# Sorted-block attention and a two-layer FFN in one kernel: seven pairs of output tiles by seven block products, scores on 64-row tiles, and the last chunk in two halves

## The chip, the cores and the metric

The kernel runs on one core of a Trainium2 chip. The metric is the device time in microseconds of one execution. The core has five instruction streams that run beside each other and wait for each other by semaphores: TensorE (PE, matmuls, with its weight loads listed as PEld), VectorE (DVE), ScalarE (ACT), GpSimd (POOL, which here also issues the loads) and SyncE (SP, which issues stores and DMA transposes).

## What is computed

```python
# q, k, v: (4, 8, 768, 64); sort_net: (4, 8, 8, 8)
P = sort_net
for _ in range(5):                       # row and column normalisation
    P = P - max(P, -1);  P = exp(P)
    P = P / (sum(P, -1) + 1e-9);  P = P / (sum(P, -2) + 1e-9)
k_sorted = einsum('bhij,bhjcd->bhicd', P, k_blocks)    # 8 blocks of 96 rows
v_sorted = einsum('bhij,bhjcd->bhicd', P, v_blocks)
scores = q_block @ k_sorted_block.T / 8                # within each block of 96
attn = softmax(scores) @ v_sorted_block                # (4, 8, 768, 64)
x = attn, heads side by side                           # (3072, 512)
h = x @ w_in                                           # w_in (512, 2048)
g = max(h, 0) + alpha * min(h, 0)                      # alpha (2048,)
out = g @ w_out                                        # w_out (2048, 512), float32
```

## The kernel before

**The work.** There are 32 attention groups g (4 batches b of 8 blocks i, 96 tokens, all 8 heads). Batch 0 is prepared in its own way; for batches 1 to 3 the sorted K and V come from matmuls against block-diagonal matrices (`prep_k` at L672, `prep_v` at L713) whose weights POOL or ACT lay out first (`conv_k` at L659, `conv_v` at L405, into the zero-padded buffers KSz and VDz). `attention` makes the scores of 8 heads (L763 in batch 0, L760 in the others), the row maxima on DVE (L769), the exponentials on ACT (L797), turns them by a DMA transpose, multiplies with V (L817), scales (L830) and turns the result into xT, the tokens as columns.

**Scores.** In batch 0 a head takes 64 rows of the matrix: two heads stand one above the other (`hp`), so the eight matmuls are four pairs on 64-row tiles. In batches 1 to 3 the two heads of a pair share the keys' 128 rows, and q is stored twice as wide, with zeros in the half of the other head (QN, zeroed by eight POOL memsets at L495; QTz by DMA transposes of 128x1024, L443): eight matmuls of all 128 rows.

**FFN.** The first layer runs in chunks of tokens: two of 192, then seven of 384. A step `ffn1` (L879) makes one of 16 blocks of 128 features (four matmuls of 384 columns; in a chunk of 192 two blocks, eight matmuls of 192), alternately into the two banks of psH; ACT (L889) and DVE (L893) apply the activation and write hT, a ring of 768 tokens. The second layer makes 24 tiles of 128 tokens. A plain tile (`ffn2`, L919) is 16 matmuls of 512 columns into one bank, a copy on ACT or DVE, and a store. A **pair** of tiles (`strassen`) is a 2x2 block product by seven products instead of eight: the blocks are the two tiles, the even and odd feature blocks, and the two halves of the 512 columns. Eight sums S of hT blocks (L994, 128x512 each, on DVE or POOL), seven products of eight matmuls of 256 columns (L1013, in two halves of four), three snapshots of partial sums (L405 into `sn`), three totals (L1027) and two stores. `w_sums` (L957) makes eight sums of w_out blocks once. PAIRS is [13, 16, 19, 22]: tiles 13, 14, 16, 17, 19, 20, 22 and 23 go by pairs, the other 16 by the plain form.

**Order.** No engine's order comes from the program text. `SEQ` is one written list of operation numbers (`_Graph` numbers them as they are added); each engine takes its operations in the list's order. A letter behind a number names the engine where there is a choice (p POOL, a ACT, d DVE; without a letter, the first of the choices: DVE for S and w_out sums, ACT for copies). `i4H` and the like are warming matmuls (L1172). `arrange` works out start times by the program's own cost figures, and `emit` places the waits that the data need.

```python
PAIRS = [13, 16, 19, 22]
SMALL = ("dve", "pool")
chunks = [(0, 2), (2, 4)] + [(c, c + 4) for c in range(4, NG, 4)]
```

Of the kernel before, what the change touches and what calls it, by code (L numbers as in the profile page):

```python
# [7 lines left out]
AP = bass.AP  # L8
# [13 lines left out]
RING = 768  # L22
# [10 lines left out]
0 18 1 4 2 7 3 8 42 43 25 10 44 5 33 40 45 46 24 11 37 47 6 48 49 14 50 51 39 52 28 53 9 54 23 55 i1P 143 56  # L33
57 i4H 26 58 29 127 59 60 61 62 21 63 126 64 41 65 66 22 85 67 128 68 87 69 83 88 70 13 71 i6Y 72 86 73 74 75
129 16 76 77 78 134 79 81 80 130 34 82 96 89 12 38 91 90d 94 95 97d 144 92 98 140 100 84 i9Y 20 101 136 103a
102d 104 17 99d 107a 110 93d 106 105d 111 145 112 108a 146 114 109 154 115 113d 147 15 155 116 148 137 120
117d 118 156 139 119 121d 122 35 157 19 132 124 123d 135 i3Y 125 27 133 158 149 159 i4G 150 160d 151 179 161
180 i2H 152 162d 153 181 36 163 182 188 164 165 166 196 189 205 190 197 192 206 183 191 193 198 207 194 209
184 195 199 185d 213 210 208 186 211 214 221 212 233 187 217 222 138 244 218 215 30 216 200 245 167p 223 201
219 232 202d 248 224 230 246 203 220 142 204 247 266 249 267 258 231 237 234 250 259 251 268 235 141 260 168  # L40
225 269 262 131 261 226 238 227d 263 252 236 239 264 241 286 315d 289 276 228 265 242 305 243 240 253 306 229
280 290 270 279 277 271 293 291 278 272d 287 307 294 292 173 275 295 273 308 170 274d 285 281 297 288 282d 314
296 342 174 283 343 309 284 301 298 310 175 316 311d 302 344 317 299 300 312 345 303 320 313d 328 326 304 321
323d 346 329 332 32 347 169p 348d 324 333 254 353 319 330 331 349 334 255 171p 350 367 335 325 318 382 256 392
383 322 351 393 395 384 394 336 31 352d 365 337 366 357 396 385 416 327 397 398 417 419 399 257 338 176 420
418 400 421 355 422 356d 425 358d 423 339 426 424 428 401 340 427 359 446 354 360d 449 429 447 361 450 368
362d 430 408 451 369 448 409 363 455 364d 431 411 458 456 452 459 410 177 386 453 370 387 457 460 439 388d 371
454 389 479 390d 372 461 402 414 403 488 443 415 404d 476 178 489 480 405 412 477 440 512 406 481 490 438 478
432 485 441d 413 482 433 434d 486 469 513 491 483 487 435 442 484 444 436 509 445d 472 462 510 524 463 506
464d 378 511 470 507 465 377 514 471 466d 508 374 521 525 518 380 522 492 523 519 515 375 526 493 520 379 545  # L50
516d 474 381 542 475 527 560 376 546 554 561 543 468 341 555 544 562 547 473 500 548 501d 499 551 494d 563 502
552 498 556 503d 549 553 535 589 557 550 534 391 590 504 577 505 558d 437 580 578 495 579 581 538 625 591 571
407 496d 582 572 583 533 537 528 586 529 584 530d 536 539 626 585 587 540 569 588 592 531 541 622 532 570d 575
631 623 573 624 627 600 574 172 632 576 598 634 599 601 564 635 602 608 565 628 633 603 610 636 637 609 629
566d 497 606 604 638 655 605d 607 517 639 567 640 373 568d 649 641 611 593 650 652 612 594 595d 656 653 651
642 596 657 597d 654 613 661 643 664 662 667 663 665 658 559 666 684 668 659 676 687 685 696 686 688 677 669
689 697 711 682 690 680 670 702 691 678 693 703 698 467 694 679 683d 704 644 695 699 810 645 692 712 722 646d
660 700 705 713 681 731 714 719 732 723 817 717 720 751 724 744 733 721 728 812 671 725 715 672 729 673d 734
766 718 745 730 752 726 767 647 816 742 706 753 727 618 768 707 674 708d 757 716 743d 748 740 758 754 749 759
741 801 750 755 746 630 621 802 763 747 769 735 619 764 760 736 737d 709 789 776 761 765 803 762 790 813 738  # L60
775 783 777 811 784 786 778d 615 836 785 787 791 620 788 779 792 614 780d 837 795 781 804 793 782d 796 797 798
770 830 799 838 800 814 815d 818 821 819 617 839 771 616 844 944p 772d 822 845 820 773 831 864 823 824 825 847
865 756 827 805 848 648 832 945p 826 828 829 866 875 849d 852 855 833 806 807d 851 853 846 872 840 850 874 856
873 854 857 858 834d 876 710 861 859 877 883 841 675 878 860 862 863 952p 948p 879 880 842d 867 889 701 890
898 774 881 899 884 891 885 868 739 900 953 808 895 950p 882 954p 869 886 924 896 887 843 870d 892 949p 925
912 893 913 871 926 901 897 894 955p 909 910 906 835 982 911 962 921 907 908 927 951p 922 983 923 918 914 919
984 902 956 957p 920 903 794 963 935 915 1002 936 904d 937 1003 916 932 928 933 1004 960 961 934 941 938 942
958p 929 959p 964d 930d 965 966 943 967 946p 939 1022 968 940 993 985 990 1023 969 888 994 986 991 995 1024
992 905 970 972d 809 999 996 947p 987 971 931 997 988d 973 974 1000 1068p 1048 998 1010 1001 917 1013 1069p
975 1011 1014 976 1049 1005 1006 978 1076 1015 1070p 1012 979 1050 1007 1019 1020 980 1016 1008d 1021 1025 989  # L70
1017 1036 1026 1018 1009 1098 1099 977 1033 1034 1030 1031 1035 1032 1027 1071p 1037 1028d 1038 1042 1100 1043
1045 1044 1046 1039 1072p 1118 1056 1040 1051 1073p 1047 1119 1059 1074p 1077 1057 1052 1078 1060 1058 1062
1075 1061 1053 1080 1101 1079 1054d 1041 1065 981 1063 1082 1083 1120 1066 1102 1081 1064 1084 1088d 1106 1107
1067 1089 1121 1090 1109 1110 1108 1111 1091 1103 1112 1029 1085 1086 1113 1168p 1087 1114 1115 1104d 1126
1116 1117 1127 1144 1128 1105 1122 1123 1129 1124d 1130 1132 1133 1145 1131 1134 1055 1135 1092 1136 1138 1137
1146 1141 1094 1095 1169p 1125 1139 1142 1140 1150 1143 1153 1151 1154 1172p 1147 1152 1148 1155 1170p 1156
1157 1159 1096 1174p 1158 1160 1176 1161 1177 1162 1180 1165 1163 1182 1164 1166 1167 1171p 1178 1097 1179
1173p 1198 1199 1181 1201 1183 1228 1200 1202 1203 1204 1188d 1207 1205 1184 1208 1206 1185 1236p 1210 1209
1211 1213 1189 1190 1234p 1186 1214 1212 1215 1175 1187 1191 1192 1149 1216 1219 1217 1194 1195 1220 1218 1222
1221 1193 1225 1093 1235p 1223 1242 1226 1196 1237p 1224 1229 1243 1244 1227 1245 1238 1246d 1248 1239 1240p  # L80
1249 1247 1250 1251 1254d 1255 1256 1257 1252 1253 1230 1231 1197 1258 1241 1259 1232d 1260 1261 1233 1262
1263
""".split()
XLAT = {"pe": 215, "act": 36, "dve": 36, "pool": 80, "sync": 80}
# [7 lines left out]
def t_act(n):  # L92
    return 170 + n / 1.2
# [1121 lines left out]
```

## Time and profile before

| | |
|---|---|
| runs shown | 231.94, 233.15, 234.76 us; median 233.15 |
| profiled execution | 231.46 us, span from the first to the last instruction 229.7 us |
| PE, DVE, ACT, POOL busy | 220.6, 175.4, 154.6, 148.2 us |
| granted TensorE clock | 1.00 throughout |
| HBM | 27.28 MB read, 6.29 MB written |
| POOL's DMA queue (loads) | 24816 packets, 44.5% of 16 engines' time |
| SP's DMA queue (stores, transposes) | 48400 packets, 37.1% |

How rows are read: a group row has the line, the engine, the operation, output<-inputs with shapes and the count, then busy microseconds and the mean nanoseconds of one, then the engine's idle time ahead of the group and who ended it. A row in order of time has the start and the length in microseconds; matmuls are pipelined, and the length of a group of them reaches into the next one. A row of stages has the stretch, its length, and then the busy time of PE, PEld, DVE, ACT and POOL with counts, the granted clock, the mean busy share of the DMA engines and GB/s. A row of the chain has start, length and engine of one piece of work on the path that ended last.

### The profile page before, as it was taken

To read this page: it belongs to the slowest core of one execution; us is meant where nothing else is said; L and a number is where in the kernel's file an instruction comes from. 1 tells how busy PE (TensorE), PEld (TensorE's weight loads), DVE (VectorE), ACT (ScalarE), POOL (GpSimd) and SP (SyncE) were. 2 spreads that over 40 slices of the span, in tenths; PEclk is the share of its full clock that TensorE was granted. 3 is DMA by queue.
4 is the path that set the end of the run, shared out by engine and by line. 5 is a ranking of instruction groups with operands and counts; after the bars stand their busy time and mean duration, and the time that the engine had idled before them with its cause. 6 is when DMAs were issued, how large, how long until landed. Compare 5 with 4: busy or idle time off the path is not lost.

```text
span 229.7 us, 6502 instructions
## 1 busy us (share of the span) xinstructions
PE 220.6 (96%) x2623; PEld 147.1 (64%) x2623; DVE 175.4 (76%) x362; ACT 154.6 (67%) x416; POOL 148.2 (65%) x182
## 2 busy tenths in 40 slices
PE   3999999999999999999999999999999999999994
PEld 3467588685666666565566566656776676566782
DVE  5659599897798979777678789668888767665753
ACT  4369667889989686867897587687676764454410
POOL 7999129859165995873989997896870604186120
PEclk9999999999999999999999999999999999999999
DMA  5999999998997399999759998954662522020213
GB/s 64 215 212 201 217 204 190 179 197 105 195 190 145 48 121 155 195 187 189 152 119 133 142 99 176 193 112 134 145 142 54 152 55 54 17 93 3 99 41 137
DMA packets 73247, 31.39 MB, mean 137 GB/s; under 512 B 64496, under 2 KB 68096, under 8 KB 73216
## 3 DMA queue, kind: packets, MB, share of 16 engines
q0 software_dynamic: 24816, 13.63, 44.5%
q1 hardware_dynamic: 48400, 17.33, 37.1%
q8 instruction: 21, 0.34, 0.6%
q14 instruction: 10, 0.08, 0.1%
HBM read 27.28 MB, written 6.29 MB: 146 GB/s over the span
## 4 chain that ended last, share of the span: by engine, by line
PE 76%; POOL 11%; DMA 9%; issue 1%; DVE 0%; POOLq 0%
PE psH L879 32%; PE psYP L919 21%; PE psYP L1013 11%; DMA KS<-in_k_dram 9%; PE psS L760 3%; POOL KSz L659 3%; PE psO L817 3%; PE psYP L713 2%; PE psYP L672 2%; PE psS L919 2%; POOL VDz L405 1%; POOL QN L495 1%; POOL w_in_bf L1077 1%; POOL QN L435 1%; PE psO L852 1%
## 5 line engine op out<-in xcount | busy, mean ns | idle before, releaser
L879 PE MATMUL psH<-xT,w_in_bf 128*128 128x384 bf16 (+1 forms) x560 | 96.7, 310 | 0.3 <-DVE hT L893 0.3
L893 DVE SCALAR_TENSOR_TENSOR hT<-t,omaT,psH 128x384 bf16<-128x384 f32 (+1 forms) x140 | 77.3, 567 | 22.3 <-ACT t L889 21.4
L889 ACT ACTIVATE t<-psH 128x384 f32<-128x384 f32 x126 | 61.0, 495 | 37.2 <-PE psH L879 34.8
L879 PEld LDWEIGHTS psH<-xT,w_in_bf 128*128 128x128 bf16 x560 | 49.9, 98 | 25.1 <-DVE hT L893 1.7
L919 PE MATMUL psYP<-w_out_bf,hT 128*128 128x512 bf16 x240 | 60.2, 379 | 0.0
L797 ACT ACTIVATE Esb<-psS,nf 96x96 bf16<-96x96 f32 x192 | 46.3, 345 | 1.6 <-DVE nf L769 1.6
L405 POOL COPY VDz<-VST 64x384 bf16<-64x384 bf16 x40 | 33.9, 848 | 16.4 <-PE psYP L713 12.2
L919 PEld LDWEIGHTS psYP<-w_out_bf,hT 128*128 128x128 bf16 x240 | 21.6, 98 | 19.4
L659 POOL COPY KSz<-KS 64x512 bf16<-64x512 bf16 x36 | 22.1, 613 | 14.3 <-DMA KS<-in_k_dram 8.6
L769 DVE TENSOR_REDUCE nf<-psS 96x8 f32<-96x768 f32 x24 | 22.8, 950 | 7.1 <-PE psS L760 6.9
L830 DVE TENSOR_TENSOR xq<-psO,rec 96x512 bf16<-96x512 f32 x30 | 20.5, 684 | 0.7
L435 POOL DMA_DIRECT2D QN<-in_q_dram x24 | 19.9, 846 | 0.7 <-POOL QN L495 0.6
L994 POOL TENSOR_TENSOR QTz<-hT 128x512 bf16<-128x512 bf16 x7 | 8.1, 1156 | 16.5 <-DVE hT L893 15.7
L994 POOL TENSOR_TENSOR VDz<-hT 128x512 bf16<-128x512 bf16 x7 | 8.1, 1153 | 15.6 <-DVE hT L893 15.3
L817 PEld LDWEIGHTS psO<-VS,ET 112*128 112x128 bf16 x248 | 11.3, 98 | 3.5 <-ACT xT L405 0.5
L817 PE MATMUL psO<-VS,ET 112*128 112x65 bf16 x248 | 12.7, 194 | 0.0
L760 PEld LDWEIGHTS psS<-KT,QTz 128*128 128x128 bf16 (+1 forms) x192 | 10.7, 101 | 3.1 <-ACT Esb L797 0.2
L760 PE MATMUL psS<-KT,QTz 128*128 128x96 bf16 (+1 forms) x192 | 12.2, 206 | 0.0
L405 DVE CAST VS<-psYP 112x512 bf16<-112x512 f32 x15 | 10.3, 687 | 2.3 <-PE psYP L713 2.3
L713 PEld LDWEIGHTS psYP<-BDV,VDz 128*128 128x128 bf16 x192 | 8.4, 98 | 3.3 <-POOL VDz L405 0.4
L405 ACT ACTIVATE outstg<-psYP 128x512 f32<-128x512 f32 x12 | 7.2, 601 | 4.4 <-PE psYP L919 4.4
L405 ACT ACTIVATE KT<-psYP 128x512 bf16<-128x512 f32 x13 | 7.8, 598 | 3.2 <-PE psYP L672 3.0
(180 smaller groups left out, 299.8 us busy)
## 6 DMA issues: line engine op xcount, KB each, us to landing
out_dram<-outstg SPq DMA_DIRECT2D x24, 256.0 KB, 2.4
KS<-in_k_dram POOLq DMA_DIRECT2D x3, 768.0 KB, 9.1
QN<-in_q_dram POOLq DMA_DIRECT2D x24, 96.0 KB, 4.1
w_in_bf<-in_moe_w_in_dram POOLq DMA_DIRECT2D x4, 512.0 KB, 17.0
w_out_bf<-in_moe_w_out_dram POOLq DMA_DIRECT2D x2, 1024.0 KB, 18.7
VST<-in_v_dram POOLq DMA_DIRECT2D x4, 384.0 KB, 10.3
hT<-in_q_dram POOLq DMA_DIRECT2D x1, 768.0 KB, 7.3
VST<-in_v_dram POOLq DMA_DIRECT2D x1, 768.0 KB, 12.6
```

The lines of the kernel that those rows point to most:

```text
L405: return e.activation(o, i, ACTF.Copy) if e is nc.scalar else e.tensor_copy(o, i)
L435: G.add(POOL, lambda e, h=h: e.dma_start(AP(QN, h * 128 + (h // 4) * 64, [[6144, 128], [1024, 6], [1, 64]]), AP(q.tensor, b * HB + h * S * ...
L659: G.add(POOL, lambda e, hp=hp: e.tensor_copy(AP(KSz, hp * 64 * 3072 + u % 3 * 1024 + hp * 64, [[3072, 64], [128, 8], [1, 64]]), AP(KS[n], ...
L760: inst = e.matmul(o, AP(QTz[n], hp * 3072 + h4 * 768 + i * 96, [[6144, 128], [1, w]]), AP(KT[n], (h4 * 8 + i) * bk, [[ld, 128], [64, 2], [ ...
L769: G.add(DVE, lambda e: e.tensor_reduce(AP(nx, 0, [[8, 96], [4, 2], [1, 4]]), AP(psX, 0, [[1024, 96], [512, 2], [96, 4], [1, 96]]), AxisLis ...
L797: inst = e.activation(AP(Esb[me], p * 128, [[1024, 96], [64, 2], [1, 48]]), AP(psX, (p // 4) * 512 + (p % 4) * 96, [[1024, 96], [48, 2], [ ...
L817: inst = e.matmul(AP(psZ, hp * 512 + h4 * 68, [[1024, 128], [1, 65]]), AP(ET[me] if far else ET[m], pos(h4, hp) * 96, [[800, nk], [1, 128] ...
L879: inst = e.matmul(AP(pt, poff + x * n, [[1024, 128], [1, n]]), AP(w_in_bf, kt * DFF + (ft + x) * 128, [[KT_TILES * DFF, 128], [1, 128]]), ...
L889: G.add(ACT, lambda e: e.activation(AP(t1[tb], 0, [[384, 128], [1, k * n]]), AP(pt, poff, [[1024, 128], [1, k * n]]), ACTF.Relu, scale=-1. ...
L893: G.add(DVE, lambda e, x=x: e.scalar_tensor_tensor(out=AP(hT, (ft + x) * RING + tok % RING, [[FT_TILES * RING, 128], [1, n]]), in0=AP(t1[t ...
L919: inst = e.matmul(AP(bank[0], bank[1], [[1024, 128], [1, n]]), AP(hT, ft * RING + tok % RING, [[FT_TILES * RING, 128], [1, 128]]), AP(w_ou ...
L1013: inst = e.matmul(AP(psYP, off, [[1024, 128], [1, 256]]), sa, mb, start=begin and j == 0, stop=j == 7, skip_group_check=True)
```

## The change

- **Pairs.** PAIRS becomes 10, 12, ..., 22: seven pairs, tiles 10 to 23; tiles 0 to 9 stay plain. Pairs take turns between two sets of buffers; the first set is now its own (`Sm`, `sn`). Pair 10 works in one bank, the last two in other banks than the rest.
- **Scores.** q is kept without the zero halves (QN and QTz half as large, the eight memsets gone, each of the 18 transposes half as large); batches 1 to 3 take the form of batch 0, on 64-row tiles.
- **Last chunk.** 2688 to 3072 becomes two chunks of 192 tokens. The ring of hT grows to 1024, with a written place for each chunk.
- **Lists anew.** SEQ is replaced. The warming matmuls are the same seven entries. In the new numbering `w_sums` is 822 to 829; the sums of the pairs are 830-837, 930-937, 1040-1047, 1110-1117, 1172-1179, 1234-1241 and 1296-1303. The numbers among these with a p are 828, 829, 834, 835, 831, 832, 836, 833; 930, 932 to 937; 1040 to 1044 and 1046, 1047 without 1045; 1110 to 1115 and 1117; 1172, 1174 to 1179; 1234 to 1241 without 1239; 1296 and 1297.

```diff
-    PAIRS = [13, 16, 19, 22]
+    PAIRS = {10: 0, 12: 1, 14: 0, 16: 1, 18: 0, 20: 1, 22: 0}
+    CHUNKS = [(0, 192, 0), (192, 384, 192), (384, 768, 384), (768, 1152, 0), (1152, 1536, 640),
+              (1536, 1920, 256), (1920, 2304, 640), (2304, 2688, 0), (2688, 2880, 384), (2880, 3072, 576)]
...
-    QN = sb("QN", [128, 6, 8, 128], BF16)
+    QN = sb("QN", [128, 6, 512], BF16)
-    QTz = [sb("QTz%d" % n, [128, 2, 4, S], BF16) for n in range(2)]
+    QTz = [sb("QTz%d" % n, [128, 4, S], BF16) for n in range(2)]
...
-            AP(QTz[n], t * 128, [[6144, 128], [768, 8], [1, 128]]),
-            AP(QN, t * 1024, [[6144, 128], [1, 1024]])),
+            AP(QTz[n], t * 128, [[3072, 128], [768, 4], [1, 128]]),
+            AP(QN, t * 512, [[3072, 128], [1, 512]])),
...
-        for h in range(H):
-            G.add(POOL, lambda e, h=h: e.memset(
-                AP(QN, h * 128 + (1 - h // 4) * 64, [[6144, 128], [1024, 6], [1, 64]]), 0.0),
-                400, w=[("QN0", h)], prio=-21)
...
-                    if far:
-                        inst = e.matmul(o, AP(QTz[n], hp * 3072 + h4 * 768 + i * 96, [[6144, 128], [1, w]]),
-                                        AP(KT[n], (h4 * 8 + i) * bk, [[ld, 128], [64, 2], [1, 48]]))
-                    else:
-                        inst = e.matmul(o, AP(QTz[n], hp * 64 * 6144 + h4 * 768 + i * 96, [[6144, 64], [1, w]]),
-                                        AP(KT[n], hp * 64 * ld + (h4 * 8 + i) * bk, [[ld, 64], [64, 2], [1, 48]]))
+                    inst = e.matmul(o, AP(QTz[n], hp * 64 * 3072 + h4 * 768 + i * 96, [[3072, 64], [1, w]]),
+                                    AP(KT[n], hp * 64 * ld + (h4 * 8 + i) * bk, [[ld, 64], [64, 2], [1, 48]]))
...
+        own = (psYP, 0, ["psY"]), (psYP, 512, PSP)
+        bx, bz_, by = {20: (own[0], own[1], (psO, 0, ["psO0"])),
+                       22: ((psS, 0, ["psS0"]), (psS, 512, ["psS1"]), (psO, 512, ["psO1"]))}.get(ta, (own[0], own[one - 1], own[one - 1]))
...
-        product(0, ["psY"], True, ((0, 0), (0, 0)))
-        product(512, PSP, True, ((0, 1), (1, 0)))
+        product(bx, 0, True, ((0, 0), (0, 0)))
+        if not one:
+            c11()
         snap(0)
-        total(outstg[oa][:, 0:256], 1, 512, 0, [("out", oa)])
-        product(0, ["psY"], False, (2, 2))
-        product(512, PSP, True, ((1, 1), 4))
-        product(768, PSP, False, (1, 1))
+        if not one:
+            total(outstg[oa][:, 0:256], 1, bz_, 0, 0, [("out", oa)])
+        product(bx, 0, False, (2, 2))
+        if not one:
+            c21()
         snap(1)
-        product(0, ["psY"], False, (3, 3))
+        product(bx, 0, False, (3, 3))
         snap(2)
...
-    chunks = [(0, 2), (2, 4)] + [(c, c + 4) for c in range(4, NG, 4)]
+    for t0, t1_, _ in CHUNKS:
```

The end of the new list is below. 1292 is the last first-layer step on PE; of the numbers behind it 1304, 1245, 1252, 1305, 1253, 1255, 1256, 1310, 1311, 1313, 1314, 1317, 1260, 1318, 1315, 1261, 1306, 1307, 1322 and 1323 are half products, 1324 is the last total and 1325 the last store.

```
1292 1304 1289 1296p 1293 1245 1290 1294 1252 1305 1201
1253 1308 1255 1297p 1256 1295 1291 1300 1301 1310 1257d 1241p 1311 1302 1258 1313 1247 1316 1299 1314 1317
1237p 1260 1318 1259 1315 1303 1261 1319d 1320 1262 1306 1307 1322 1263 1321 1323 1309 1324 1325
```

More of the change, by code (lines that the diff above doesn't have):

```diff
@@ L380, in bass_sinkhorn_attn__then__act_prelu_kernel @@
     xq = [sb("xq%d" % n, [96, 512], BF16) for n in range(NE)]
-    t1 = [sb("t1%d" % n, [128, 384], F32) for n in range(3)]
+    t1 = sb("t1", [128, 1152], F32)
+    Sm = sb("Sm", [128, 4096], BF16)
+    sn = sb("sn", [128, 768], F32)
     outstg = [sb("outstg%d" % n, [128, DM], F32) for n in range(4)]
@@ L864, in bass_sinkhorn_attn__then__act_prelu_kernel, with place, grains, ffn1 @@
     ffn_ops = []
-    def ffn1(ga, gb, ft, prio):
-        tok, n = ga * BLK, (gb - ga) * BLK
-        tb = step[0] % 3
-        banks = BANK_H + ([BANK_P] if ga < 2 else [])
+    def place(tok):
+        for t0, t1_, at in CHUNKS:
+            if t0 <= tok < t1_:
+                return at + tok - t0
+    def grains(tok, n):
+        return [y // 64 for y in range(place(tok), place(tok) + n, 64)]
+    def ffn1(tok, end, ft, prio):
+        n = end - tok
+        tb = step[0] % 2 * 512 if n == 512 else step[0] % 3 * 384
+        kt1 = [("t1", y) for y in range(tb // 128, (tb + max(n, 384)) // 128)]
+        banks = BANK_H + ([BANK_P] if tok == 0 else [])
         pt, poff, _, keys = banks[step[0] % len(banks)]
@@ L883, in f @@
             return inst
-        op = G.add(PE, f, t_pe(*[(n, 128)] * (4 * k)), r=[("xT", g % 16) for g in range(ga, gb)] + [("w_in", ft // 8 * 2 + x) for x in range(2)],
+        op = G.add(PE, f, t_pe(*[(n, 128)] * (4 * k)), r=[("xT", g % 16) for g in range(tok // BLK, (end - 1) // BLK + 1)] + [("w_in", ft // 8 * 2 + x) for x in range(2)],
                    w=keys, prio=prio)
@@ L924, in ffn2 @@
                 op = G.add(PE, f, t_pe(*[(n, 128)] * 4),
-                           r=[("hT", ft, y) for ft in range(4 * part, 4 * part + 4) for y in grains]
+                           r=[("hT", ft, y) for ft in range(4 * part, 4 * part + 4) for y in grains(tok, 128)]
                            + [("w_out", part // 2)], w=key, prio=prios[part] + x)
```

208 lines of the change are left out of this document (109 added, 99 removed).

## The prediction

> **What bounds the kernel now.** I read first the page's busy times and its chain, then the stages, and only then the order of the matmuls.
>
> ```profile
> PE 220.6 (96%) x2623; PEld 147.1 (64%) x2623; DVE 175.4 (76%) x362; ACT 154.6 (67%) x416; POOL 148.2 (65%) x182
> PE 76%; POOL 11%; DMA 9%; issue 1%; DVE 0%; POOLq 0%
> ```
>
> PE is busy 96% of the span and holds 76% of the chain that ends last; DMA and POOL hold the rest. The stages say where (stretch, its length, then busy time of PE, weight loads, DVE, ACT, POOL, each with a count, then clock, DMA share, GB/s):
>
> ```profile
> 5.00:20.00 15.00, 13.37 (x247) 7.93 (x248) 10.41 (x38) 9.38 (x20) 14.52 (x21) 1.00 1.11 209
> 20.00:35.00 15.00, 14.74 (x278) 11.36 (x277) 12.20 (x30) 10.65 (x25) 5.93 (x10) 1.00 1.13 210
> 17.60:50.00 32.40, 30.87 (x602) 24.46 (x602) 28.74 (x67) 25.06 (x50) 20.11 (x29) 1.00 1.36 195
> 50.00:226.60 176.60, 176.55 (x1644) 114.55 (x1644) 135.60 (x248) 120.71 (x349) 112.11 (x125) 1.00 0.72 123
> ```
>
> From 50 us to 226.6 us PE has 176.55 us of 176.60: no wait is left there, and the clock is 1.00. Only the start has gaps, and 1.53 us of these lie between 17.6 and 50. So a change is worth, one for one, the PE work that it takes out after 50 us, less any wait that it newly makes, plus at most 1.5 us from the start. A busy PE might still hide slow matmuls, so each price is taken from start to start of neighbouring groups.
>
> ```profile
> 107.00 0.50 PE L760 MATMUL psS<-KT,QTz 128*128 128x96 bf16 x8
> 107.34 1.03 PE L919 MATMUL psYP<-w_out_bf,hT 128*128 128x512 bf16 x4
> 108.20 1.46 PE L879 MATMUL psH<-xT,w_in_bf 128*128 128x384 bf16 x8
> 109.50 1.89 PE L919 MATMUL psYP<-w_out_bf,hT 128*128 128x512 bf16 x8
> 111.23 0.40 PE L713 MATMUL psYP<-BDV,VDz 128*128 128x64 bf16 x8
> 219.24 4.80 PE psYP L1013 x44
> ```
>
> The first five are from the order of time; the durations there overlap the next group, the differences of the starts don't. Eight full-row score matmuls take 107.34 - 107.00 = 0.34 us; four of 512 columns (111.23 - 109.50)/2 = 0.865; two first-layer steps of 384 columns 1.30, so one 0.65. The last row is from the chain: 44 block products' matmuls of 256 columns in 4.80 us, so 0.436 for a half product of four.
>
> **The change, part by part.**
>
> *More pairs.* Before, 4 pairs go by seven products and 16 tiles by the plain form; after, 7 pairs and 10 tiles (0 to 9). Six tiles leave L919: 6 x 4 x 0.865 = 20.76 us. Three pairs come: 3 x 7 x 2 = 42 half products x 0.436 = 18.31 us. On PE, **-2.45 us**, all after 50 us, where PE decides.
>
> *Scores on 64-row tiles.* The 24 groups of batches 1 to 3 lose the zero halves and take the form that batch 0 has already at L763. That form stands in the trace beside other work:
>
> ```profile
> 28.17 0.83 PE L879 MATMUL psH<-xT,w_in_bf 128*128 128x192 bf16 x8
> 28.93 0.34 PE L763 MATMUL psS<-KT,QTz 64*128 64x96 bf16 x8
> 29.21 0.83 PE L879 MATMUL psYP<-xT,w_in_bf 128*128 128x192 bf16 x8
> 29.88 0.82 PE L879 MATMUL psH<-xT,w_in_bf 128*128 128x192 bf16 x8
> 30.54 0.41 PE L817 MATMUL psO<-VS,ET 112*128 112x65 bf16 x8
> 30.90 0.34 PE L785 MATMUL psS<-QTz,KT 64*128 64x96 bf16 x8
> 102.90 0.41 PE L817 MATMUL psO<-VS,ET 112*128 112x65 bf16 x8
> 103.15 0.81 PE L879 MATMUL psH<-xT,w_in_bf 128*128 128x384 bf16 x4
> ```
>
> From its own start to the next group's it takes 29.21 - 28.93 = 0.28 us, 0.06 less than 0.34. But the group ahead of it grows: the 192-column step takes 0.76 us ahead of L763 and (30.54 - 29.21)/2 = 0.665 ahead of others, and L817 takes 0.36 ahead of L785 and 0.25 ahead of L879. Going over to 64-row tiles costs 0.095 to 0.11 us, paid by the neighbour. I take 0.28 + 0.095 - 0.34 = +0.035 a group, x 24 = **+0.84 us**. The ends: +1.2 at 0.11, and -1.44 if the switch were free. The Trainium skill, TensorEngine Tiling (Array Packing), Key Properties, says that a change of the tiling mode drains the engine; the 0.095 us agree.
>
> *Last chunk split.* 16 steps of 384 columns (10.40 us) become 16 steps of twice 4 matmuls of 192, 16 x 0.665 = 10.64 us: **+0.24 us**. Its weight loads double, but the 0.665 was measured with them. DVE gets 32 passes at L893 instead of 16.
>
> *Smaller transposes, no memsets, same DMAs.* The q loads stay 24 on POOL's queue with the same bytes; the 18 transposes on SP's queue carry half, and their landing is early enough now (PE waits for nothing after 50 us), so nothing. Eight memsets of QN leave POOL in the first 24 us:
>
> ```profile
> L495 POOL MEMSET QN<- 128x384 bf16 x8 | 3.5, 442 | 0.1
> 11.77 21.16 DMA KS<-in_k_dram
> ```
>
> Six of them stand ahead of the issue of batch 1's K at 11.77 us, on which the chain then waits 21.16 us. I take nothing, since the DMA share is 1.11 and 1.13 at 209 and 210 GB/s from 5 to 35 us (packets overlap, so it can pass 1), already full ahead of that transfer: it is late for the bytes before it, not for its issue. The other end is -1.5 us, all gaps of PE from 17.6 to 50.
>
> *What the pairs put on DVE, ACT and POOL.* By the letters in the list the sums of the 7 pairs fall 43 on POOL and 13 on DVE (before 25 and 7), and of the eight sums of w_out two on POOL and six on DVE (before all on POOL).
>
> ```profile
> L957 POOL TENSOR_TENSOR WT<-w_out_bf 128x1024 bf16<-128x1024 bf16 x2 | 4.3, 2126 | 0.2
> L994 POOL TENSOR_TENSOR QTz<-hT 128x512 bf16<-128x512 bf16 x7 | 8.1, 1156 | 16.5 <-DVE hT L893 15.7 <-DVE QTz L994 0.6
> L994 DVE TENSOR_TENSOR VDz<-hT,VDz 128x512 bf16<-128x512 bf16 x2 | 0.8, 418 | 0.0
> 219.15 0.83 DVE L994 TENSOR_TENSOR VDz<-hT 128x512 bf16<-128x512 bf16 x1
> L1027 DVE TENSOR_TENSOR outstg<-psYP,QTz 128x512 f32<-128x512 f32 x2 | 1.4, 692 | 0.3 <-PE psYP L1013 0.3
> L1027 DVE TENSOR_TENSOR outstg<-psYP,QTz 128x256 f32<-128x256 f32 x4 | 1.6, 406 | 0.2 <-PE psYP L1013 0.2
> ```
>
> POOL: 18 x 1.156 - 6 x 2.126 - 3.5 = +4.5 us, beside PE; from 170 us on it is mostly idle. DVE: totals 3 x (0.69 + 2 x 0.41) = 4.5, last chunk about 3, sums 6 x 0.42 = 2.5, and the six sums of w_out, which the trace never shows on DVE: twice the 512-column sum, 0.84 each, or 1.65 by the row at 219.15, so 5.0 to 9.9. Together +15 to +20 us. Hidden, as long as L893 empties psH in time:
>
> ```profile
> 65.00:80.00 15.00, 15.00 (x173) 9.59 (x172) 13.53 (x28) 11.90 (x38) 11.93 (x15) 1.00 0.71 121
> 110.00:140.00 30.00, 30.00 (x314) 18.50 (x313) 23.80 (x42) 23.71 (x77) 27.34 (x33) 1.00 0.95 128
> 140.00:170.00 30.00, 30.00 (x273) 19.67 (x271) 23.33 (x45) 22.46 (x72) 24.66 (x19) 1.00 0.73 152
> ```
>
> DVE at 13.53 of 15 us cost PE nothing from 65 to 80, and the new work goes mostly where DVE has 23.8 and 23.3 of 30. I take 0 us of new waits. Queued behind a late sum on DVE would be L893, behind that the next first-layer step on PE.
>
> *End.* The chain's last pieces, from its last first-layer steps on, and two groups of the page:
>
> ```profile
> 216.64 1.30 PE psH L879 x8
> ...
> 225.77 0.89 PE psYP L1013 x8
> 226.66 0.02 issue
> 226.68 0.42 DVE outstg L1027
> ...
> L889 ACT ACTIVATE t<-psH 128x384 f32<-128x384 f32 x126 | 61.0, 495 | 37.2 <-PE psH L879 34.8
> L893 DVE SCALAR_TENSOR_TENSOR hT<-t,omaT,psH 128x384 bf16<-128x384 f32 (+1 forms) x140 | 77.3, 567 | 22.3 <-ACT t L889 21.4
> ```
>
> After PE's last matmul, at 226.66, come one DVE total and one store, to 229.7; the same two stand last in the new list. After the last first-layer step PE has 226.66 - 217.94 = 8.7 us of work now, and the new list gives it 20 half products there, 8.7 us again, so the late sums of pair 22 have the same cover. Nothing; without that cover, PE would wait for the passes at L889 and L893 and one sum on DVE, 0.50 + 0.57 + 0.42 = 1.5 us.
>
> **Sum:** -2.45 + 0.84 + 0.24 = **-1.4 us**. The profiled execution, 231.46 us (span 229.7 and 1.76 around it), would take 230.1. It lies 1.7 below the median of the three runs; on the median, 233.15 becomes **231.8 us**.
>
> **The rivals.**
>
> *DVE holds PE up; slower.* A w_out sum has two inputs in SBUF, as the L994 sum has that took 0.83 us while POOL ran its own sum:
>
> ```profile
> 218.54 1.15 POOL L994 TENSOR_TENSOR VDz<-hT 128x512 bf16<-128x512 bf16 x1 [5.08 <-DVE hT L893]
> ```
>
> The DVE sum began at 219.15, inside POOL's 218.54 to 219.69; the six that ran without POOL took 0.41 or 0.42. Between 100 and 145 us POOL copies VST and KS nearly all the time (27.34 of 30). If each of the six sums is 0.81 us longer and holds up L893, and by it PE, by as much, the price is 6 x 0.81 = 4.9, the net +3.5 us: 236.6. It turns the sign from 1.4 us of waits on, two sums of the six. For it: POOL's load there. Against it: two psH banks, and the 13.53 of 15. In the Trainium skill, SBUF — State Buffer, Who interferes with whom, a DVE instruction with two SBUF inputs contends with a GpSimd one that reads SBUF, and the loser waits in full; by this rule the 0.83 is no accident, and the trace agrees with it. Half the price gives 234.2.
>
> *The 64-row tiles save PE time.* If going over were free, -1.44 instead of +0.84: 229.5. Against it stand both rows of 0.76 and 0.36. The same page of the skill, under Theoretical Speedup, promises up to 2x where a dimension is at most 64. As a mechanism of this kernel, halving 0.34 in 24 groups is -4.1, in all -6.3: 226.9; the trace speaks against it, since the group alone takes 0.28.
>
> *The start gets shorter.* Without the memsets K of batch 1 is issued up to 2.6 us earlier; were it to land so, PE's 1.5 us of gaps go: -2.9, 230.3. Against it: the full DMA from 5 us on.
>
> **How the numbers follow.** About 1% is what a measurement of this kernel can tell from no change: runs of the kernel before lie between 231.94 and 234.76. Forecast (-2 to -0.7 us): 0.60. DVE late: 0.20, half of it over 1%. Tiles save: 0.08 (0.02 of it halved). Shorter start: 0.12. One per cent is 2.3 us. The forecast falls within 1% unless the medians stray by a further 1 us, which I give 0.12 of its 0.60 on the fast side and 0.04 on the slow one; two rivals add 0.13 to faster. So faster 0.25, same 0.60, slower 0.15. The range goes from the free switch, 229.4, to a little over half the price of the DVE rival, 234.7; what is left out is the full price and the halved groups.
>
> **What would show it.** Right: L919 at 160 matmuls and L1013 at 392, by 0.216 and 0.109 each; the score group 0.28 with 0.095 on its neighbour; PE's busy time from 50 us to its end with no gap, and its end near 225.3. Wrong: idle before L879 released by L893 between 100 and 170 us, DVE sums of 128x1024 at 1.6 us, PE waiting for L994 on POOL, or batch 1's K landing before 32 us.

## The result, and the profile after

The changed kernel takes **238.89 us** (median of four runs, 238.81 to 241.15); the kernel before, on the same chip, 232.55 (231.80 to 234.76). The ratio is 1.032 [1.027, 1.036]: slower, where 231.8 was forecast, and outside the range of 229.4 to 234.7. The profiled execution is the longest of the four, 241.15 us with a span of 239.4. Only it has a trace; the other three are 2.2 to 2.3 us shorter, at the same mean granted clock of 0.986, and which of the waits below is shorter in them isn't shown.

The page of the kernel after, its busy times and its chain:

```profile
PE 220.8 (92%) x2743; PEld 154.3 (64%) x2759; DVE 188.0 (79%) x396; ACT 157.8 (66%) x429; POOL 154.2 (64%) x186
PE 58%; DMA 17%; POOL 16%; SPq 4%; issue 2%; DVE 2%; ACT 0%; POOLq 0%
```

PE is busy as long as before (220.6), but holds 58% of the chain instead of 76%; DMA, POOL and SP's queue have the rest. The stages of the kernel after, with the columns as before:

```profile
50.00:104.00 54.00, 53.49 (x566) 32.15 (x571) 46.04 (x85) 44.02 (x126) 36.58 (x51) 1.00 0.90 126
104.00:111.90 7.90, 5.63 (x46) 2.57 (x43) 6.00 (x10) 6.51 (x24) 0.15 (x1) 1.00 1.20 139
111.90:119.30 7.40, 2.74 (x19) 1.33 (x20) 0.89 (x2) 0.57 (x2) 7.24 (x10) 0.85 1.49 202
119.30:124.00 4.70, 4.68 (x38) 2.73 (x39) 2.10 (x4) 2.84 (x10) 4.43 (x6) 0.51 0.50 51
148.00:156.00 8.00, 6.73 (x72) 4.37 (x71) 7.39 (x12) 4.80 (x13) 7.61 (x6) 1.00 0.68 133
156.00:236.10 80.10, 80.10 (x772) 64.45 (x770) 65.21 (x135) 44.09 (x133) 43.68 (x38) 1.00 0.32 73
```

From 156 us to PE's end PE has no gap, as was forecast for all that follows 50 us. The loss lies between 104 and 124 us: PE idles 2.27 us of the second stretch and 4.66 of the third, and runs the fourth at a granted clock of 0.51. A smaller gap of 1.27 us lies between 148 and 156. The waits, who waited for whom, total, times, longest:

```profile
PE psYP L715 <- POOL VDz L411: 4.6, 1, 4.6
PE psO L815 <- DMA ET<-Esb: 2.3, 1, 2.3
PE psH L886 <- DVE hT L900: 1.5, 2, 1.3
POOL QN L441 <- DMA QTz<-QN: 9.1, 1, 9.1
```

And the chain through that place, in order of time:

```profile
99.40 11.87 DMA QTz<-QN
111.26 0.48 issue
111.75 2.48 POOL QN L441 x3
...
115.85 0.83 POOL QN L441
116.68 0.83 POOL VDz L411
...
119.32 0.61 PE psYP L715 x8
```

The last transpose of batch 2's q takes 11.87 us to land. POOL has next the q loads of batch 3 (L441), which overwrite what that transpose reads; it waits 9.1 us, and only then lays out V of batch 3 (L411), for which PE waits. In the kernel before the same transpose is issued at another time:

```profile
113.38 1.31 SPq L443 DMA_TRANSPOSE QTz<-QN  x1
```

There it lands 3.2 us later, though it carries twice the bytes; it stands behind all loads of batch 3's V and K, and POOL has its q loads behind most of the copies of V. The new lists issue it at 99.40, in the middle of these loads. Most of the V loads lengthen too. The issue to landing of the four, in the kernel before and then in the kernel after:

```profile
DMA to landing us min/median/max: 5.2/6.4/7.2
```

```profile
DMA to landing us min/median/max: 4.1/8.4/9.7
```

The half clock is seen in PE's order of time behind the wait:

```profile
121.60 1.91 PE L925 MATMUL psYP<-w_out_bf,hT 128*128 128x512 bf16 x4
123.31 0.65 PE L815 MATMUL psO<-VS,ET 112*128 112x65 bf16 x8
```

From start to start four matmuls of 512 columns take 1.71 us, twice the 0.865 of the prediction. The six groups from 119.32 to 124.07 take 4.75 us; the same six take 2.65 in e12 below, whose clock is 1.00, so the half clock costs 2.1. Together 2.34 (L815) + 4.56 (L715) + 2.1 (half clock) + 1.27 (L886) = 10.3 us; the forecast for this execution, 230.1, and these give 240.4 of the 241.15.

### The profile page after: what moved, and what is told of

Same layout as the page of the kernel before. It is cut to its first block, busy times and chain, and to the rows that moved or that the text cites. A ratio compares the mean times of both kernels' runs of the same rounds, so it can differ in the third digit from the quotient of the medians.

```text
span 239.4 us, 6812 instructions
## 1 busy us (share of the span) xinstructions
PE 220.8 (92%) x2743; PEld 154.3 (64%) x2759; DVE 188.0 (79%) x396; ACT 157.8 (66%) x429; POOL 154.2 (64%) x186
## 4 chain that ended last, share of the span: by engine, by line
PE 58%; DMA 17%; POOL 16%; SPq 4%; issue 2%; DVE 2%; ACT 0%; POOLq 0%
PE psH L886 25%; PE psYP L1024 14%; DMA KS<-in_k_dram 10%; PE psYP L925 7%; DMA QTz<-QN 5%; POOL QN L441 5%; POOL VDz L411 4%; POOL KSz L661 3%; SPq L449 3%; DMA QN<-in_q_dram 3%; PE psO L1024 2%; PE psO L815 2%; PE psS L761 2%; PE psYP L715 2%; PE psS L1024 1%
## 5 line engine op out<-in xcount | busy, mean ns | idle before, releaser
L886 PE MATMUL psH<-xT,w_in_bf 128*128 128x384 bf16 (+1 forms) x624 | 98.5, 297 | 1.6 <-DVE hT L900 1.5
L886 PEld LDWEIGHTS psH<-xT,w_in_bf 128*128 128x128 bf16 x624 | 54.4, 98 | 23.3 <-DVE hT L900 2.9
L411 POOL COPY VDz<-VST 64x384 bf16<-64x384 bf16 x40 | 33.9, 846 | 14.7 <-PE psYP L715 12.7
L925 PE MATMUL psYP<-w_out_bf,hT 128*128 128x512 bf16 x144 | 37.7, 386 | 0.9
L767 DVE TENSOR_REDUCE nf<-psS 96x8 f32<-96x768 f32 x24 | 22.8, 950 | 10.8 <-PE psS L761 10.8
L999 POOL TENSOR_TENSOR Sm<-hT 128x512 bf16<-128x512 bf16 x12 | 13.9, 1159 | 20.8 <-DVE hT L900 20.2
L441 POOL DMA_DIRECT2D QN<-in_q_dram x24 | 20.1, 852 | 9.1 <-DMA QTz<-QN 9.1
L925 PEld LDWEIGHTS psYP<-w_out_bf,hT 128*128 128x128 bf16 x160 | 14.2, 99 | 12.9 <-issue 0.9
L999 POOL TENSOR_TENSOR VDz<-hT 128x512 bf16<-128x512 bf16 x11 | 13.1, 1195 | 8.8 <-DVE VDz L999 3.9
L815 PE MATMUL psO<-VS,ET 112*128 112x65 bf16 x248 | 12.9, 196 | 2.3 <-DMA ET<-Esb 2.3
L815 PEld LDWEIGHTS psO<-VS,ET 112*128 112x128 bf16 x248 | 11.3, 99 | 5.9 <-DMA ET<-Esb 2.7
L715 PE MATMUL psYP<-BDV,VDz 128*128 128x64 bf16 x192 | 9.8, 196 | 4.6 <-POOL VDz L411 4.6
L411 ACT ACTIVATE VS<-psYP 112x512 bf16<-112x512 f32 x13 | 9.0, 692 | 7.0 <-PE psYP L715 6.9
L1024 PE MATMUL psYP<-w_out_bf,hT 128*128 128x256 bf16 x96 | 13.3, 273 | 0.0
L715 PEld LDWEIGHTS psYP<-BDV,VDz 128*128 128x128 bf16 x192 | 8.3, 100 | 7.5 <-POOL VDz L411 5.2
L761 PEld LDWEIGHTS psS<-KT,QTz 64*128 64x128 bf16 (+1 forms) x248 | 6.6, 99 | 8.4 <-ACT t L896 3.3
L761 PE MATMUL psS<-KT,QTz 64*128 64x96 bf16 (+1 forms) x248 | 11.0, 208 | 0.5 <-DVE KT L411 0.4
```

The source lines that it names most:

```text
L411: return e.activation(o, i, ACTF.Copy) if e is nc.scalar else e.tensor_copy(o, i)
L441: G.add(POOL, lambda e, h=h: e.dma_start(AP(QN, h % 4 * 128 + h // 4 * 64, [[3072, 128], [512, 6], [1, 64]]), AP(q.tensor, b * HB + h * S ...
L715: inst = e.matmul(AP(t, off + dd * 64, [[row, 128], [1, 64]]), AP(VDz, (u % VSL * 8 + dd) * 128, [[VSL * 1024, 128], [1, 128]]), AP(BDV, b ...
L815: inst = e.matmul(AP(psZ, hp * 512 + h4 * 68, [[1024, 128], [1, 65]]), AP(ET[me] if far else ET[m], pos(h4, hp) * 96, [[800, nk], [1, 128] ...
L886: inst = e.matmul(AP(pt, poff + x * n, [[1024, 128], [1, n]]), AP(w_in_bf, kt * DFF + (ft + x) * 128, [[KT_TILES * DFF, 128], [1, 128]]), ...
L925: inst = e.matmul(AP(bank[0], bank[1], [[1024, 128], [1, n]]), AP(hT, ft * RING + place(tok), [[FT_TILES * RING, 128], [1, 128]]), AP(w_ou ...
```

## The experiments

The theory is B in the expectations: a transposing DMA and the row loads under way beside it stretch each other, and the new lists put them together and have PE ask for what they bring before its other work. Its rivals are A, only POOL's order is at fault (q loads that wait, ahead of the V copies), and C, the added compute, on DVE above all. Numbers like 459 are operations of SEQ: 459 is the late q transpose; 598 to 601 and 602 to 605 are batch 3's V and K loads, 606 to 613 its q loads; 635 is the E turn of group 16 (the transposing DMA of its exponentials) and 636 the product that reads it (L815), 674 the first `prep_v` product (L715). The lists are cut to the entries that moved and their neighbours.

### One queue at a time

**e1_q_loads_later.**

```diff
 POOL
-603 610 612 613 602 604 605 607 669 ... 673 609 707 ... 733 803 737 767 736
+603 602 604 605 669 ... 673 707 ... 733 610 803 612 737 613 767 607 736 609
```

> The changed kernel, with five of batch 3's q loads (h 4, 6, 7, 1, 3) moved on POOL behind the copies of batch 3's V, where the kernel before has them; nothing else moves. Theory A (POOL stood in order behind a q load that waits for the last q transpose, so K's loads and V's copies came late): PE's 4.6 us wait for VDz and the stretch at half clock behind it go, some 6 to 7 us, so 231 to 234 us, with the 2.3 us wait for ET still there. Theory B (transposes and loads that run beside each other slow each other, wherever POOL stands): little goes, 236 us or more. Theory C (the added work on DVE): no gain, 238 to 239.

Measured: 237.77 us, ratio 1.025 [1.021, 1.029].

```profile
PE psO L815 <- DMA ET<-Esb: 7.1, 2, 6.4
```

The V copies no longer queue behind a waiting load, and PE's wait at L715 is gone. But the wait only moves to the E turn: with POOL free to issue the K loads at once, the late transpose takes 12.6 us, the V loads up to 11.0. **Rival A falls** as the whole cause.

**e2_transpose_earlier.**

```diff
 SP
-584 489 509 365 459 635
+584 459 489 509 365 635
```

> The changed kernel, with one entry of SyncE's order moved: the transpose of q tile 3 of batch 2 stands ahead of that of tile 4 and of two stores, so that the last transpose is issued near 97.9 us and not 99.4, before V's loads begin to move at 99 us. Theory A: it lands in 3 to 4 us, POOL waits no 9 us, and most of 7 us go: 231 to 234 us. Theory B: the same or better, since less runs beside the loads. Theory C: 238 to 239. If the transpose still lands near 111 us, A gains nothing by it: 238.

Measured: 234.72 us, 1.013 [1.010, 1.017]. Issued at 98.1 instead of 99.4, ahead of most loads, the transpose lands in 7.1 us, not 11.9; PE waits 2.0 us for the E turn, and runs at half clock behind it. The stage behind that wait, its granted clock 0.50:

```profile
113.50:116.00 2.50, 2.50 (x16) 1.28 (x16) 0.00 (x0) 0.37 (x1) 2.31 (x4) 0.50 2.01 90
```

A little over half of the loss is gone by one entry of a list.

**e6_queues_as_before** (e1's POOL order, and the transpose as late as in the kernel before).

```diff
 SP
-365 459 635 662 622
+365 635 662 459 622
```

> The changed kernel, with both queues at this place in the order of the kernel before: the last q transpose of batch 2 is issued behind the exponentials' transpose of group 17, after the V and K loads, and five q loads of batch 3 stand on POOL behind V's copies. All of the change's computation stays. Theories A and B both say that the loss at 105 to 125 us goes: the prediction's -1.4 us and up to 1.3 for the DVE sum of w_out at 151 us remain, 230.3 to 232 where the kernel before has 231.7. If 235 or more stays, the change's own work costs it.

Measured: 237.31 us, 1.025 [1.022, 1.028].

```profile
PE psO L815 <- DMA ET<-Esb: 4.4, 1, 4.4
```

A miss for the theory as it then stood: the late q transpose is out of the way (5.3 us to land), but the E turn of group 16, issued at 104.8 beside the K loads, now takes 9.4 us. It is not the late q transpose alone that is slow there.

**e5_loads_after_transposes.** The V loads wait for the late transpose (tile 3) instead of that of tile 5, and 601 stands behind 459 in the list.

```diff
-                r=[("QTzt", 0, 5)] * (b == 3), w=[("VST", b % 2)] * (x == 0) + [("VST", b % 2, x)],
+                r=[("QTzt", 0, 3)] * (b == 3), w=[("VST", b % 2)] * (x == 0) + [("VST", b % 2, x)],
```

> The changed kernel, with batch 3's V loads made to wait for the last q transpose of batch 2 in SyncE's order (tile 3) instead of tile 5, and one copy of K moved ahead of the first V load on POOL. Transposes and V loads no longer overlap. Theory B (a q transpose that is under way beside the V and K loads stretches all of them): the transpose lands in 3 us instead of 11.9, the V loads in 5 to 7 us, though issued 3 to 4 us later; PE's waits for ET and VDz shrink: 231 to 234 us. Theory A (POOL's order alone): POOL still meets the q loads ahead of K's, but now the transpose has landed, so it gives about the same; if loads that start later bring V later, 235 or more.

Measured: 243.71 us, 1.053 [1.047, 1.059]. Kept apart, both are quick: the transpose lands in 2.7 us, the V loads in 3.3 to 6.1. But the last K copy of batch 2, which the edit was to bring ahead, still stood on POOL behind the V load that now waits, which cost PE 4.0 us (L674), and the loads, moved later, met the next E turn: 10.1 us to land and 4.7 us of wait. That is a miss for the 231 to 234 us expected: the edit moved the collision, and as a cure it says nothing.

### The collision put into the kernel before

**e8_before_transpose_moved** moves that one transpose in the kernel before, **e3_before_queue_order** POOL's q loads as well (618, 620, 621 ahead of 612; 615 behind 613).

```diff
 SP (kernel before)
-373 643 ... 670 467 660
+373 467 643 ... 670 660
```

> The kernel before, with one entry of SyncE's order moved: the last q transpose of batch 2 is issued near 99.5 us, behind the two stores, beside the V loads, and not at 113.4. POOL's order is untouched, so no q load stands ahead of K's loads or V's copies. Theory B: the V loads land 3 to 8 us later, PE waits for VDz, 236 us or more (up to 245, as when both queues were changed). Theory A: no loss, 231.5 to 232.5.

> The kernel before, with only its queues in the changed kernel's order at this place: SyncE issues the last q transpose of batch 2 right behind the stores at 98 us, and POOL has three q loads of batch 3 ahead of the last two of K's four loads and a fourth ahead of V's copies. No pair, score group or chunk is changed. Theory A: POOL stalls and PE waits as in the changed kernel, 237 to 241 us. Theory C: no loss, 232 to 233. Theory B alone: 1 to 3 us lost.

Measured: e8 234.64, 239.40, 240.42 and 242.91 us; e3 232.90, 241.13, 247.96 and 247.97; the kernel before 231.6 to 231.7 (medians). The rows are of the longest run of each: e8, then e3, then the landing of e8's V loads:

```profile
PE psYP L713 <- POOL VDz L405: 8.7, 1, 8.7
```

```profile
PE psYP L713 <- POOL VDz L405: 13.2, 1, 13.2
```

```profile
DMA to landing us min/median/max: 4.8/16.0/16.1
```

One transpose, issued at 101 instead of 113, lands in 18.9 us and holds the loads beside it to 16, where they took 5.2 to 7.2. The wait of 8.7 us and some 2.6 us of half clock behind it make up the 11.3 us that this run has over the kernel before; its granted clock is 1.00 up to 115 us and from 126 us on. So one moved entry costs a kernel without any other part of the change 3.0 us in the quickest of four runs and 11.3 in the longest. The other runs have no trace, so why they differ so much, and why e3's quickest loses only 1.2 us, isn't shown.

### The bytes, and their control

**e13_quarter_loads.** Batch 3's V and K loads bring a quarter of their columns; lists untouched.

```diff
-                AP(VST[b % 2], th * 64 * 3072 + c, [[3072, 64], [1, t]]),
+                AP(VST[b % 2], th * 64 * 3072 + c, [[3072, 64], [1, t // (4 if b == 3 else 1)]]),
... (the source and load_kv alike)
```

> The kernel after, its lists untouched, but the loads of batch 3's V and K bring only a quarter of their columns (so batch 3 is computed from stale rows): the same instructions in the same order with a quarter of the bytes beside the transposes. Theory B: the last query transpose, issued at 99.4, lands in about 4 us and not 11.9, the V loads in about 3, the E turn of group 16 in about 4; POOL's copies of V are 4 to 5 us earlier; the waits at L715 (4.6) and L815 (2.3) and the half clock go: about 231. Rival A (POOL's order alone, the query loads that wait ahead of the copies of V): the same, as far as the transpose lands early; what tells them apart is e1, where the order alone changed little. Rival C (compute): 238, no change. If a transpose's landing depends only on its place in SP's queue and not on bytes beside it: 11 to 12 us again and 238.

Measured: **231.74 us**, 0.999 [0.996, 1.001]. The late transpose, the V loads, and PE's longest wait in this place:

```profile
L449 SPq DMA_TRANSPOSE QTz<-QN x1: 1190/1190/1190, 101.4 to 101.4; - x1
...
DMA to landing us min/median/max: 3.9/3.9/3.9
```

```profile
DMA to landing us min/median/max: 2.6/2.8/3.4
```

```profile
PE psYP L715 <- POOL VDz L411: 1.0, 1, 1.0
```

The same instructions in the same order: the transpose (issued at 101.4 here, 2 us later than in the kernel after) lands in 3.9 us instead of 11.9, the E turn of group 16 in 2.8 instead of 7.3, the wait of 2.3 is gone, that of 4.6 is 1.0, and the clock is 1.00 from 104 to 156 us. The loss goes with the bytes; rival C would have left 238.

**e18_before_quarter_loads** does the same to the kernel before.

> Control: the kernel before, lists untouched, with the loads of batch 3's V and K cut to a quarter of their columns (batch 3 is computed from stale rows), as e13 did to the kernel after. Theory B: PE waits for none of these landings in the kernel before, so nothing: 232 within 0.5. If fewer bytes make any of these kernels faster by themselves, whatever the list (less traffic at the ports, for instance): 1 us or more faster, and e13's gain would be partly that.

Measured: 231.92 against 231.86 us, 1.002 [0.999, 1.005]. Fewer bytes alone don't make the kernel before faster, so what e13 gained is the collision.

### PE's order

**e12_product_before_wait** (on e6):

```diff
 PE
-676 636 688 689 679 674
+676 688 689 679 636 674
```

> e6 with one change of PE's order: the first product of group 16 with its turned E (L815) moved behind the two second-layer half tiles and the first-layer step that follow it (2 x 0.865 + 0.65 = 2.4 us of work). DMA queues as in e6. Theory B: the turn lands when it did (about 114), so PE's wait falls from 4.4 to 2.0 and the half-clock stretch is shorter: about 234. If the wait were not the price (compute, rival C): 237 as e6.

Measured: **232.48 us**, 1.002 [1.000, 1.005]. The E turn still takes 8.4 us, but PE has 2.4 us of work ahead of it:

```profile
PE psO L815 <- DMA ET<-Esb: 1.1, 1, 1.1
```

4.8 us under e6's 237.31 for one moved product, more than the 3.3 forecast: behind this short wait the clock stays at 1.00, so the half-clock stretch goes whole.

**e11_k_after_v_copies** (on e6): POOL's 603, 602, 604, 605 behind 707; **e14_both** adds e12's move.

> The kernel after, with queue q's entries as in e6 (the last query transpose of batch 2 issued at 110, the query loads of batch 3 behind POOL's copies of V), and besides the four K loads of batch 3 moved on POOL from ahead of the first V copies to behind the eighth. Theory B (a transposing DMA and the row loads beside it stretch each other, and this list gives PE nothing else to do meanwhile): the E turn of group 16, issued at 104.8, has only the tails of the V loads beside it and lands in about 4 us instead of 9.4, before PE asks for it at 109.8; e6's wait of 4.4 us at L815 and the half-clock stretch behind it (2.2 us) go: 231 us, so 6 less than e6, level with the kernel before. If the length of the new list's compute were the cause (rival C): no change against e6, 237. If a turn takes 9 us at that place whatever is beside it: 237.

> e11 and e12 together: queue q's entries as before, batch 3's K loads behind the eighth V copy, and group 16's product 2.4 us later in PE's order. By theory B the first leaves the second little to do: 231, within 0.5 of e11. If e11 leaves a wait of a microsecond or two, this one takes it: a microsecond or two below e11. Compute alone (rival C): 237.

Measured: 236.78 us, 1.021 [1.018, 1.023], and 236.50, 1.019 [1.015, 1.022], against 231 forecast for both. The E turn of group 16 lands in 4.2 us, as it should. But the K loads, now at 117 to 118, meet the E turn issued at 118.4 (first row), and POOL's last copies of V stand behind the issue of these four loads, 2.18 us, and behind a copy of K that waits 2.40 us for one of them to land (second row: PE's wait; both of e11):

```profile
DMA to landing us min/median/max: 7.0/7.0/7.0
```

```profile
PE psYP L715 <- POOL VDz L411: 3.0, 1, 3.0
```

A collision moved to a place where PE has as little slack is not a cure.

**e15_two_moves** (e2 and e12's move, on the kernel after) and **e16_one_step_more** (636 behind 682 as well).

> The kernel after with two list entries moved and nothing else: e2's (the last query transpose of batch 2 five places earlier on SP, issued at 98.1) and e12's (the first product of group 16 with its turned E, L815, behind the two second-layer half tiles and the first-layer step that follow it). Theory B with PE's order (the loss is the late landing and that PE asks for it before its other work): e2's wait of 2.0 at L815 and the half clock behind it (some 2 us) go: 231 to 232, against 234.7 of e2. If PE's order mattered only with queue q's entries put back as in e12: 234 to 235.

> e15 with that product moved one first-layer step and one score group further on PE (0.93 us more work ahead of it). If what e15 has left at L815 is a wait: it goes, and the time is up to 1 us under e15's, 231. If e15 has no wait left there: the same as e15 within 0.3. If the moved product makes a later one late (its softmax feeds the first layer's next step): slower than e15 by a microsecond.

Measured: 235.83 us, 1.018 [1.012, 1.023], and 234.31, 1.010 [1.006, 1.014]. Both miss the 231 to 232 us expected. The transpose went out at 99.4 again in e15's profile (SP spent 2.24 us on issuing the one ahead of it, where e2's took 1.27), landed in 9.7 us, and stretched two stores as well, to 8.9 and 9.9. ACT waited for their buffer:

```profile
ACT outstg L411 <- DMA out_dram<-outstg: 2.6, 1, 2.6
```

and PE 2.5 us for ACT's copy, ahead of L925. In e16's profile, the longest of its runs (237.17), PE waits 3.1 us for the E turn again. What work ahead covers for one transfer, another transfer of the same knot can take back, and e12's move gives nothing on e2's order.

**e17_queues_and_order** (e12 with 636 behind 682).

> e12 (queue q's entries as before, group 16's first product with its turned E behind the two second-layer half tiles and the first-layer step) with that product moved by one score group and one first-layer step more (0.28 + 0.65 = 0.93 us). e12 still waited 1.1 us there. If that wait is what is left over the forecast of 231.8: it goes, 231.4 to 231.6, so 0.9 to 1 under e12. If it is not: 232.5 as e12. If the move makes a store's buffer or a later product late, as in e15: 233 or more.

Measured: 232.81 us, 1.004 [1.002, 1.007]. The wait for the E turn is gone, but the next product now waits 1.0 us for DVE, by the profile for a row maximum (L767) behind its scaling of the first. It has about as much wait as e13 and takes 1 us longer; that difference stays unexplained.

### What the rest costs by itself

**e10_warm_in_gap** puts warming matmuls (i8P, i18P) ahead of 636 and 674 in the kernel after.

> The changed kernel, with warming matmuls (L1198's form) put into PE's two gaps: 8 ahead of group 16's attention matmuls, 18 ahead of V's first preparation of batch 3. They do nothing for the data. If the stretch at half clock (119 to 124 us at 0.51) follows from PE's idling, the clock stays at 1.00 and 2 to 2.5 us go: 236 to 237 us; the waits for ET and VDz stay, filled. If the clock falls for another reason, or the gaps are shorter than the fillers (5.6 us), 238.5 to 240.

Measured: 237.91 us, 1.029 [1.024, 1.035], clock 1.00 in the profile: the half clock follows PE's idling. Net of the added matmuls it is worth about 1 us here, which is less than the runs scatter (237.39 to 239.81) and less than the 2 to 2.5 us expected.

**e4_narrow_q_alone** gives the kernel before the narrow q, the scores on 64-row tiles and no memsets, with its own pairs and order.

> The kernel before, with only q stored without zero halves and the scores of batches 1 to 3 on 64-row tiles (its pair buffers moved out of QTz; order kept, the eight memsets left out). The prediction's price is +0.035 us for each of 24 groups, +0.84 us in all, on PE, and nothing for the memsets and the half transposes: 233.2 to 233.8 where the kernel before has 232.6. If the switch to 64-row tiles were free: 231.1. If the missing memsets shorten the start: 231 to 232.

Measured: 232.96 against 231.74 us, 1.005 [1.004, 1.007]: +1.2 us, where the prediction had +0.84 with +1.2 as its end.

## Why the prediction was wrong

**The step that failed** is the one that cost the transposes and loads at nothing: "their landing is early enough now (PE waits for nothing after 50 us), so nothing". That is true of the list before; the lists were new. The order of SP's and POOL's queues stood in the new SEQ as plainly as the letters of the sums, which were counted; that operation 459 comes 14 us earlier, beside the V loads and a K load, wasn't looked up. The trace before had rows to bound it by. The E turn at 106.3, beside the K loads, took 5.5 us against 2.8 for the one at 112. And with batch 2's V loads of 56.3 and 56.8 us under way, an E turn (issued at 57.6), a store (58.9) and a q transpose (59.5) took 8.0, 8.6 and 8.8 us; that transpose is the longest of the 18:

```profile
L443 SPq DMA_TRANSPOSE QTz<-QN x18: 1231/1320/3260, 45.1 to 163.6; - x18
...
DMA to landing us min/median/max: 3.2/3.8/8.8
```

PE had other work then and waited for none of them. What the runs showed in place of nothing: 238.89 us, 7.1 over the forecast; in the profiled execution, two waits of 4.56 and 2.34 us and 2.1 us of half clock behind them.

**The terms of PE's work held.** In the order of time of the kernel after:

```profile
162.28 0.60 PE L1024 MATMUL psYP<-KS,hT 128*128 128x256 bf16 x4
162.81 0.34 PE L761 MATMUL psS<-KT,QTz 64*128 64x96 bf16 x8
163.09 0.61 PE L1024 MATMUL psYP<-VST,hT 128*128 128x256 bf16 x4
...
169.44 1.47 PE L1024 MATMUL psYP<-w_out_bf,hT 128*128 128x256 bf16 x12
170.75 0.81 PE L886 MATMUL psH<-xT,w_in_bf 128*128 128x384 bf16 x4
```

A score group takes 163.09 - 162.81 = 0.28 us; twelve block matmuls take 1.31, so a half product 0.437 (0.436 forecast). Ahead of a score group four take 162.81 - 162.28 = 0.53, so the neighbour pays 0.09, about the 0.095 forecast. Sixteen matmuls of 192 columns take 1.32 us (206.57 to 207.89), so eight of them 0.66, as the 0.665 of the split chunk. With e4's 1.2 for the narrow form the sum is -2.45 + 1.2 + 0.24 = -1.0 us. As a shorter time, no run shows this gain: e13, with the collision taken out and a wait of 1.0 left, stands at -0.3 of 232.07, an interval that holds zero, and e12 at +0.4. DVE's added work came to 12.6 us and POOL's to 6.0, where 15 to 20 and 4.5 were forecast.

**The rivals.** *DVE holds PE up* did occur, once, by the mechanism named. The w_out sums on DVE, and POOL's at the same time:

```profile
L963 DVE TENSOR_TENSOR WT<-w_out_bf x2: 1429/1952/2475, 98.5 to 151.0; 128x1024 bf16<-128x1024 bf16 x2
L963 DVE TENSOR_TENSOR KS<-w_out_bf x2: 679/680/680, 106.8 to 135.2; 128x1024 bf16<-128x1024 bf16 x2
L963 DVE TENSOR_TENSOR VST<-w_out_bf,KS x2: 681/744/806, 107.9 to 141.8; 128x1024 bf16<-128x1024 bf16 x2
L963 POOL TENSOR_TENSOR KS<-w_out_bf,VST x1: 2122/2122/2122, 150.8 to 150.8; 128x1024 bf16<-128x1024 bf16 x1
```

The sum of 2.48 us at 151.0 runs beside POOL's 2.12, held the activation up, and PE waited 1.27 us; three of the six took 0.68, under the 0.84 assumed. The price was 1.3, not 4.9, and in e6 and e12, with other timing, no more than 0.3 is left of that wait. *64-row tiles save* fell (e4: 1.2 us slower); what this rival calls the same page of the Trainium skill is TensorEngine Tiling (Array Packing), named under the scores, and not the SBUF page named just before it. *A shorter start* fell as argued: batch 1's K was issued at 9.61 instead of 11.77, and the chain of the kernel after has

```profile
9.61 23.33 DMA KS<-in_k_dram
```

so it landed at 32.94 us, as before (11.77 + 21.16 = 32.93). It was not late for its issue; the bytes ahead of it, as the prediction argued, fit that.

**What stays open** is what, inside the DMA engines, makes a transpose and row loads stretch each other. The Trainium skill, DMA: Bandwidth & Descriptors, Issuing engines are not separate DMA queues, has DMAs of all issuing engines on the same 16 engines, interleaved. The runs agree: SP's stores and transposes and POOL's loads all lengthen together. No run here tells shared bandwidth from the order within the engines.

## What to carry over

When a change comes with new written lists, read every queue's order, not only the engine that binds: for each DMA, the time of issue, what is under way beside it, and what PE would do if it landed at twice its present time. A queue's landing times belong to its order and don't carry over to another. Another place for a transfer only moved the collision in e1, e5 and e11, and gave back a little over half of the loss in e2. What brought the time back to that of the kernel before was the old queue order together with work ahead of the consumer (e12); the same work on another queue order (e15) did not. And a wait on PE can cost more than its length: waits of 1.97, 4.41 and 4.56 us (e2, e6 and the kernel after) were followed by a stretch at half clock that cost 1.6, 2.4 and 2.1 us more.

## What the runs showed of the hardware

- Transposing DMAs and row loads stretch each other, both ways. In the kernel after and its variants, a q transpose takes 2.7 us with no load beside it (e5), 3.9 beside quarter loads (e13), 11.9 and 12.6 beside full ones (the kernel after, e1). In the kernel before, where it carries twice the bytes, it takes 3.2 us behind the loads and 18.9 among them (e8). V loads take 2.6 to 3.4 us as quarters, 3.3 to 6.1 with no q transpose beside them (e5), up to 16.1 with one (e8). Two stores took 8.9 and 9.9 (e15).
- PE falls to half clock some time after it starts to idle, and the length of the wait alone doesn't decide it. Behind e2's wait of 1.97 us, eight matmuls of 512 columns take 2.39 us from start to start (1.73 at full clock) and the next stretch is granted 0.50. In the kernel after, the product and the same eight matmuls behind the longer wait of 2.34 us take 1.98 us (111.97 to 113.95), as at full clock, against 2.65 in e2; its clock falls only at 117.1, inside the next wait. Behind e12's 1.1 us nothing is lost. The Trainium skill, TensorE: Matmul & The Clock Gate, Part 1: The HAM clock gate, puts the fall after at least one idle window of about 3.4 us; in e2 it came with 1.97 us of waiting, so here a wait well under that length can bring it.
- A DVE sum of two SBUF inputs took 0.68 us with POOL idle beside it (106.8 us) and 2.48 beside a POOL sum of 2.12.
